# Pooled attention and a softplus feed-forward layer on one core: the scores of a chunk's two tiles in one interlude, the last keys transposed in one

## The chip, the cores and the metric

The kernel runs on one core of a Trainium2 chip. The metric is the device time of one execution in microseconds. The kernel before takes 896.08 us (median of 3 runs, 895.99 to 897.66). The core's engines are TensorE (PE; PEld is its weight load), VectorE (DVE), ScalarE (ACT), GpSimd (POOL) and SyncE (SP), which issues the DMAs.

## The reference

```python
# q, k, v: (8 batches, 8 heads, 576 tokens, 64), float32
k_p = k.reshape(B, H, Sp, pool, D).mean(axis=3)      # pool = 8, Sp = 72 pooled keys
v_p = v.reshape(B, H, Sp, pool, D).mean(axis=3)
scores = scale * np.matmul(q, k_p.transpose(0, 1, 3, 2))
scores = scores - np.max(scores, axis=-1, keepdims=True)
attn = np.exp(scores)
attn = attn / (np.sum(attn, axis=-1, keepdims=True) + 1e-09)
attn_out = np.matmul(attn, v_p)
x = attn_out.transpose(0, 2, 1, 3).reshape(4608, 512)
h = x @ w_in                                         # 512 x 2048
g = np.maximum(h, 0.0) + np.log1p(np.exp(-np.abs(h)))
out = g @ w_out                                      # 2048 x 512
```

## The kernel before

The 4608 tokens are worked through in 18 chunks (c = 0 to 17) of 256 tokens, each of two tiles of 128. A chunk first has its attention computed, which gives its rows of x, and then the feed-forward layer.

The feed-forward layer is most of the work. The 2048 hidden columns are taken in 8 pairs (u = 0 to 7) of two blocks of 128. To keep float32 accuracy, each operand is split in a high and a low part, and each product is three matmuls. For a pair, `pair1` (L582, tile h) makes the first products in 24 matmuls. ScalarE takes the softplus twice (L590, L604), VectorE forms low parts and sums of quarters (L611, L641 to L644, L660), and the second products follow. From chunk 4 (NF) on these are `pair2_fast` (L730, tile m): seven products of quarters instead of eight (a Strassen-like scheme), 21 matmuls, summed over the 8 pairs in four PSUM banks. They are made in the order 1, 2, 6, 7, 5, 3, 4. Product 4 is alone in its bank, so half of that bank is free. `finish` (L743, L751) puts a chunk's output together from the seven sums. Chunk 3 uses the plain `pair2` (L623).

The attention of a tile, in class `Tile`: `qT` transposes q in four transposes (L379), `qT_out` copies them out of PSUM; `scores` makes the scores of the eight heads (L399). A head has 64 dimensions and 64 rows of the tile are taken at a time, so four small matmuls share the array: two heads (j, the even and the odd half, each into its own bank) times two halves of the rows (i). In the profile each of them is two records, so a tile's scores are 32 records. `least` takes the row minimum (the scale is negative) of a bank's four heads (L406) and `less` subtracts it (L413), on VectorE. The exponential on ScalarE runs once for both tiles. Then come the row sums (L430), the reciprocal (L434, L435), `main` (L439) for the first 64 of the 72 keys and `ends` (L446) for the last 8. `ends` writes the products of the last 8 keys three times over, as 96 columns for each half of the heads, since they are used as high, low and high part: it is two VectorE instructions a tile. `PT` transposes the first 64 keys (L460, four transposes), `last` the last ones (L472, two transposes of 96 columns), `last_high` (L479) and `last_low` (L484) split them. `av_products` (L501, L508) multiplies with the values.

What sets the order. The whole order of work is made by a planner when the kernel is built, class `Order`. Every step is an `op` with an engine, a duration, steps that it waits for (`after`), and buffers (`Slot`s of a kind, as PSUM banks). It places steps one by one: it finds the engine whose next step could end first, and of that engine's steps that could start before this one's end and at most PAUSE (0.4 us) later than its first, it takes the one with the highest rank (longest path to the end, and a bonus `first`). `HOP` (0.15 us) is added for a step's result to reach another engine. The steps are then issued in order of planned start, and each engine works in that order; the framework sets the semaphores, and orders the accesses of different engines to a PSUM bank.

There are two lists: the first for the start of the kernel with chunks 0 to 2 and the attention of chunk 3, the second for the steady part (chunks 3 to 17). In the steady list, `steady_attention(c + 1)` is added while chunk c is in work, and products are planned at MM = 0.1195 us each. PSUM's eight banks are there two for h, four for sums (kind "acc") and two for all of the attention (kind "bank"). The scores of a tile take both of the latter.

Of the kernel before, what the change touches and what calls it, by code (L numbers as in the profile page):

```python
# [30 lines left out]
class Order:  # L31
# [5 lines left out]
    AWAY = 20  # L37

    def __init__(self, kinds):
        self.ops, self.kinds, self.first, self.last, self.begin, self.table = [], kinds, 0, None, {}, None  # L40

    def op(self, engine, cost, fn, after=(), slots=(), lag=None, rest=0, first=0, table=None):
# [9 lines left out]
    def run(self):  # L52
        for o in reversed(self.ops):
            o.rank = o.cost + max([x.rank + o.lag for x in o.followers] + [o.rest])
        now = dict(self.begin)
        table = self.table

        def cost(o):
            return o.cost + (self.TABLE if o.table not in (None, table) else 0)

        free = {k: [(0, n) for n in names] for k, names in self.kinds.items()}
        left = {o.i: len(o.after) for o in self.ops}
        ready = [o for o in self.ops if not o.after]
        order = []
        while ready:
            best, could = None, []
            for o in ready:
                new = [x.kind for x in o.slots if x.name is None]
                if any(len(free[k]) < new.count(k) for k in set(new)):
                    continue  # L70
                t = max([now.get(o.engine, 0)]
                        + [x.end + (x.lag if x.engine != o.engine or x.lag > 1 else 0)
                           for x in o.after]
                        + [sorted(free[k])[new.count(k) - 1][0] for k in set(new)])
                could.append((t, o))
                if best is None or t + cost(o) < best[0]:
                    best = t + cost(o), o.engine
            by = min(t for t, o in could if o.engine == best[1]) + self.PAUSE
# [25 lines left out]
def pooled_attention_softplus_ffn(  # L104
# [266 lines left out]
    class Tile:  # L371
# [110 lines left out]
        def last_low(self, ps):  # L482
# [2 lines left out]
                out=o, in0=ps[R:2 * R, 0:2 * P].rearrange("p (a i) -> p a i", a=2),  # L485
                in1=o.bitcast(F32), op=ALU.subtract)

    def av_products(c, pss):

        pt, lt = pt_[c], last_[c]
        sp = [(b % 2, slice(lo - c * CT, hi - c * CT)) for lo, hi, b in spans(c * CT, (c + 1) * CT)]
        for g in range(2):
            for i, t in sp:
                for e in range(2):
                    for r, ps in enumerate(pss):
                        rows, n = slice(r * KM, (r + 1) * KM), 2 * g + e

                        nc.tensor.matmul(  # L501
                            out=ps[e * D:(e + 1) * D, g * CT + t.start:g * CT + t.stop],
                            lhsT=vs[i][rows, n], rhs=pt[rows, n, t],
                            start=g == 0 and t.start == 0, stop=False)
# [208 lines left out]
    def pair2_fast(c, u, which=(1, 2, 6, 7, 5, 3, 4)):  # L713
        if u == 0:
            for i in range(0, len(which), 2):
                b = psum.tile([P, DM], F32, tag=m_banks.pop(0), name="m")
                ms.setdefault(c, {}).update({n: b[:, j * O2:(j + 1) * O2]
                                             for j, n in enumerate(which[i:i + 2])})
        g, gh, gl = gs[c, u]
        so = ss[c, u][1]  # L720
        a = {n: (gh[:, i], gl[:, i]) for n, i in ((1, 0), (2, 2), (4, 1))}
# [504 lines left out]
    def steady_attention(c):  # L1226
        s_q, s_E, s_lt = Slot("q"), Slot("E"), Slot("lt_")
        tiles = [Tile(c, t) for t in range(T)]

        def load():  # L1230
            load_q(c)
        o_q = op(SYNC, 3.0, load, qT_done.get(c - 1, ()), [s_q], lag=2.4)
        subs = []
        qT_done[c], score_done[c], av_done[c], x_done[c] = [], [], [], []
        for x in tiles:
            sp = spans(x.first, x.first + P)
            s, s_qT, s_mn = Slot("bank"), Slot("qT"), Slot("mn")
# [3 lines left out]
            o = op(ACT, act(512), lambda x=x, s=s, n=s_qT: x.qT_out(s.tile, n.name),  # L1241
                   [o], [s, s_qT])
            last, ss = [], [Slot("bank"), Slot("bank")]
            p = op(PE, 0.7, lambda x=x, ss=ss: x.scores([bank(s, "sc") for s in ss]),
                   [o, *parts_of(sp, k_ready)], [s_qT, *ss], first=EARLY)
            score_done[c].append(p)
            for i, s in enumerate(ss):
                last = [op(DVE, 0.46, lambda x=x, i=i, s=s, n=s_mn: x.least(i, s.tile, n.name), [p, *last],
                           [s, s_mn])]

                def less(x=x, i=i, s=s):
                    if c not in e_:
                        new_E(c)
                    x.less(i, s.tile)
                subs.append(op(DVE, 0.46, less, last, [s, s_mn, s_E]))
        return lambda where: probabilities(c, tiles, s_E, s_lt, subs, where)

    def probabilities(c, tiles, s_E, s_lt, subs, where):

        s_pT, lows = Slot("pT"), []  # L1260
        ex = op(ACT, 1.2 + TABLE, lambda: exponential(e_[c]), [*subs, where], [s_E])
        op(ACT, TABLE, lambda: None, [ex], first=5000)
        for x in tiles:
            s_sm, s_pm, s_pe = Slot("sm"), Slot("G"), Slot("pe")
# [3 lines left out]
            e = op(DVE, 0.52, x.ends, [o], [s_E, s_sm, s_pe])  # L1268
            s, r = Slot("bank"), Slot("bank")
            o = op(PE, 0.45, lambda x=x, s=s: x.PT(bank(s, "ptp")), [m], [s, s_pm], first=EARLY)  # L1270
            lows.append(op(ACT, act(512), lambda x=x, s=s: x.PT_out(s.tile), [o], [s, s_pT]))
            o = op(PE, 0.15, lambda x=x, r=r: x.last(bank(r, "ltp")), [e], [r, s_pe], first=EARLY)
            h = op(ACT, act(256), lambda x=x, r=r: x.last_high(r.tile), [o], [r, s_lt])
            lows.append(op(DVE, dve2(256), lambda x=x, r=r: x.last_low(r.tile), [h], [r, s_lt]))

        def values(after=()):
            sp = spans(c * CT, (c + 1) * CT)
            ss = [Slot("bank"), Slot("bank")]
            o = op(PE, 1.55 if len(sp) == 1 else 2.1,
                   lambda: av_products(c, [bank(s, "avp") for s in ss]),  # L1280
                   [*lows, *parts_of(sp, v_ready), *after], [*ss, s_lt, s_pT], first=EARLY)
            av_done[c].append(o)
# [50 lines left out]
    banks_of, drained = {}, {}  # L1333

    def second_products(c, u, before):
        fast = c >= NF
# [19 lines left out]
        elif u in (0, FP - 1):  # L1356
# [2 lines left out]
            o = p2[c, u] = op(PE, 9 * MM, lambda: fn((5, 3, 4)), [i, o], [*slots, *banks[2:]])  # L1359
            if u == FP - 1:  # L1360
                output(c, [i, o], banks)
        else:
            o = p2[c, u] = op(PE, 21 * MM, fn, wait, [*slots, *banks])
        return o
# [91 lines left out]
```

## Time and profile before

| what | value |
|---|---|
| median of 3 runs | 896.08 us |
| profiled execution, its own time | 899.16 us |
| its span, first to last instruction | 897.4 us |
| mean granted TensorE clock | 0.996 |
| TensorE busy | 884.9 us (99%) |
| first products L582, matmuls and busy time | 2880, 354.2 us |
| second products L730, matmuls | 2352 |
| scores L399, records and busy time | 1152, 27.2 us |
| transposes of the last keys L472 | 72, 14.0 us |

The span is the time between the first and the last instruction of one profiled execution; what the execution takes beyond it lies before and after. Busy time of TensorE counts each matmul from start to end, and matmuls overlap, so the sum over rows is more than the time that they hold the path. The chain of work that ended last gives each piece's share of the path, and is the better view here: its rows add up.

### The profile page before, as it was taken

What the parts mean: (1) busy time and instruction counts of PE and PEld (TensorE: products, weight loads), DVE (VectorE), ACT (ScalarE), POOL (GpSimd) and SP (SyncE); (2) the same over time, 40 slices, a digit from 0 to 9 for tenths busy, and PEclk for the clock granted to TensorE, in tenths of its full rate; (3) what the DMA queues carried; (4) which work ended last, traced back from release to release, by engine and by line L of the source; (5) the groups of instructions that cost most, each with busy time, mean ns of one, the idle gap of its engine ahead of it and who ended that gap; (6) DMA issues with size and microseconds to landing.
All of it is one profiled execution on the core that took longest, in us unless ns stands there. A gap on an engine that the chain in (4) does not pass through costs nothing.

```text
span 897.4 us, 20505 instructions
## 1 busy us (share of the span) xinstructions
PE 884.9 (99%) x8308; PEld 836.9 (93%) x8308; DVE 649.4 (72%) x1601; ACT 408.0 (45%) x824; POOL 2.4 (0%) x19
## 2 busy tenths in 40 slices
PE   7999999999999999999999999999999999999997
PEld 4789989888999999999999999999999999999997
DVE  5899999888867678787677666777566565747454
ACT  4964333445353544454444444353545354434332
POOL 1000000000000000000000000000000000000000
PEclk8999999999999999999999999999999999999999
DMA  8975545545897678687668775776656565747472
GB/s 247 283 245 179 198 144 166 171 156 180 283 291 232 225 244 263 201 267 235 211 199 256 230 221 190 221 245 219 221 171 229 188 212 190 234 142 228 173 241 88
DMA packets 107085, 191.12 MB, mean 213 GB/s; under 512 B 46064, under 2 KB 60400, under 8 KB 106992
## 3 DMA queue, kind: packets, MB, share of 16 engines
q1 hardware_dynamic: 106992, 189.82, 65.3%
q8 instruction: 65, 1.06, 0.5%
q14 instruction: 28, 0.23, 0.1%
HBM read 167.25 MB, written 22.54 MB: 211 GB/s over the span
## 4 chain that ended last, share of the span: by engine, by line
PE 95%; DMA 2%; DVE 1%; ACT 1%; SPq 0%; issue 0%; DVEq 0%; ACTq 0%
PE h L582 36%; PE m L730 30%; PE acc L556 7%; PE h L534 7%; PE acc L623 3%; PE sc L399 2%; PE avp L501 2%; PE qTp L379 2%; PE ptp L460 2%; PE avp L508 2%; DMA l<-wi 1%; PE ltp L472 1%; PE kps L965 1%; DMA kvl<-in_v_dram 1%; DMA kvst<-in_k_dram 0%; ACT E L424 0%
## 5 line engine op out<-in xcount | busy, mean ns | idle before, releaser
L582 PE MATMUL h<-x,l 128*128 128x256 f32 x2748 | 337.6, 279 | 0.5 <-DMA l<-wi 0.5
L582 PEld LDWEIGHTS h<-x,l 128*128 128x128 f32 x2748 | 323.8, 188 | 1.2 <-DMA l<-wi 0.7
L590 ACT ACTIVATE g<-h 128x512 f32<-128x512 f32 x120 | 71.9, 599 | 281.4 <-PE h L582 281.3
L730 PE MATMUL m<-w,so 128*128 128x256 f32 x1134 | 147.8, 277 | 0.0
L730 PEld LDWEIGHTS m<-w,so 128*128 128x128 f32 x1134 | 137.8, 188 | 0.1
L641 DVE TENSOR_TENSOR sf<-g 128x128 f32<-128x128 f32 x112 | 32.7, 292 | 127.4 <-ACT g L590 126.8
L655 ACT CAST so<-sf 128x512 fp32r<-128x512 f32 x112 | 69.7, 623 | 58.0 <-DVE sf L644 56.8
L660 DVE TENSOR_TENSOR so<-sf,so 128x512 fp32r<-128x512 f32 x112 | 77.4, 691 | 23.0 <-ACT so L655 22.9
L730 PE MATMUL m<-w,gh 128*128 128x256 f32 x476 | 91.5, 281 | 0.0
L730 PEld LDWEIGHTS m<-w,gh 128*128 128x128 f32 x476 | 71.9, 188 | 0.0
L611 DVE TENSOR_TENSOR gl<-g,gh 128x384 fp32r<-128x384 f32 (+1 forms) x120 | 67.3, 561 | 0.4 <-ACT gh L604 0.4
L730 PE MATMUL m<-w,gl 128*128 128x256 f32 x238 | 66.0, 277 | 0.0
L604 ACT ACTIVATE gh<-h 128x384 fp32r<-128x384 f32 (+1 forms) x120 | 59.1, 492 | 0.0
L539 ACT ACTIVATE g<-h 128x256 fp32r<-128x256 f32 x96 | 32.0, 382 | 55.4 <-PE h L534 33.5
L534 PEld LDWEIGHTS h<-x,w 128*128 128x128 f32 x396 | 48.6, 188 | 2.7 <-ACT g L539 0.6
L534 PE MATMUL h<-x,w 128*128 128x256 f32 x396 | 49.8, 278 | 0.2 <-ACT g L539 0.2
L730 PEld LDWEIGHTS m<-w,gl 128*128 128x128 f32 x238 | 44.7, 188 | 0.0
L751 DVE TENSOR_TENSOR o<-o,m 128x256 f32<-128x256 f32 x98 | 39.8, 418 | 3.3 <-ACT o L743 0.4
L556 PE MATMUL acc<-w,g 128*128 128x512 f32 x132 | 41.9, 399 | 0.0
L730 PE MATMUL m<-l,gh 128*128 128x256 f32 x196 | 39.9, 292 | 0.0
L406 DVE TENSOR_REDUCE mn<-sc 128x4 f32<-128x288 f32 x72 | 31.4, 451 | 7.9 <-PE sc L399 7.6
L644 DVE TENSOR_TENSOR sf<-g,sf 128x128 f32<-128x128 f32 x112 | 32.7, 292 | 3.9
(198 smaller groups left out, 1252.8 us busy)
## 6 DMA issues: line engine op xcount, KB each, us to landing
l<-wi SPq DMA_DIRECT2D x224, 512.0 KB
out_dram<-o SPq DMA_DIRECT2D x36, 256.0 KB
q<-in_q_dram SPq DMA_DIRECT2D x32, 256.0 KB
kst<-in_k_dram SPq DMA_DIRECT2D x24, 288.0 KB
vst<-in_v_dram SPq DMA_DIRECT2D x24, 256.0 KB
stage<-in_moe_w_in_dram SPq DMA_DIRECT2D x22, 256.0 KB
stage<-in_moe_w_out_dram SPq DMA_DIRECT2D x11, 512.0 KB
wi<-w SPq DMA_DIRECT2D x11, 512.0 KB
```

The lines of the kernel that those rows point to most:

```text
L534: nc.tensor.matmul(out=ps[:, 0:CT], lhsT=row(w, kc), rhs=x[:, kc], start=first and kc == j == 0, stop=last and kc == KC - 1 and j == 2)
L556: nc.tensor.matmul(out=accs[c][t], lhsT=a[:, ts], rhs=w, start=f == 0 and j == 0, stop=f == FC - 1 and j == 2)
L582: nc.tensor.matmul(out=ps[:, k * CT:(k + 1) * CT], lhsT=row(w, kc), rhs=x_[c][i][:, kc], start=first and n == 0, stop=last and n == len(or ...
L590: nc.scalar.activation(out=g, in_=x.rearrange("p (b i) -> p b i", i=P), func=AF.Softplus)
L604: nc.scalar.activation(out=gh, in_=quarters(c, x.rearrange("p (b i) -> p b i", i=P)), func=AF.Softplus)
L611: nc.vector.tensor_tensor(out=gl, in0=quarters(c, g), in1=gh.bitcast(F32), op=ALU.subtract)
L641: tt(out=sf[:, 2], in0=g[:, 0], in1=g[:, 2], op=ALU.add)
L644: tt(out=sf[:, 3], in0=g[:, 3], in1=sf[:, 1], op=ALU.subtract)
L655: nc.scalar.copy(out=so[:, 0], in_=ss[c, u])
L660: nc.vector.tensor_tensor(out=so[:, 1], in0=sf, in1=so[:, 0].bitcast(F32), op=ALU.subtract)
L730: nc.tensor.matmul(out=ms[c][n], lhsT=x, rhs=y, start=u == 0 and j == 0 and n in (1, 6, 5, 4), stop=u == FP - 1 and j == 2 and n in (2, 7, ...
L751: nc.vector.tensor_tensor(out=o, in0=in0, in1=m[n], op=how)
```

## The change

It touches the second (steady) list.

- The scores of both tiles of a chunk are one step, `pair_scores`, and take three banks instead of two at a time for each tile. The bank of half j takes seven heads (tile 0's four and tile 1's first three); the two heads left, tile 1's last pair, go in the first 144 columns of a third bank. For chunks 4 and 5 the third is a bank of kind "acc"; from chunk 6 on it is the free half of the bank of product 4 of chunk c - 2 (`ms[...]["rest"]`), written without the flag that starts a sum.
- The order of the scores' matmuls is: tile 1's last even head, all of tile 0, the rest of tile 1, tile 1's last odd head. A GpSimd memset of a small tile waits for the first of these, and the last of these waits for the memset.
- Minima and subtractions follow the banks: `pair_least` three times (two over 504 elements, one over 144), `pair_less` seven times, in place of four and four. The third bank's come first, with the bonus HURRY.
- The last keys: `pair_ends` writes each tile's products once (128x64, one VectorE instruction a tile), `pair_last` transposes both tiles' in one step of two transposes, `pair_high` makes the copies of the high part in four ScalarE copies (two of a tile's `last_high` before), `pair_low_ends` the low part in two.
- Durations in the list: MM is 0.1142 us instead of 0.1195, PAUSE for TensorE is 0.1 us instead of 0.4, av_products 1.7 and 2.15 instead of 1.55 and 2.1.

```diff
+    def pair_scores(c, tiles, pss):
+        rest, own = pss[2]
+        last = HP - 1
+        order = [(tiles[1], last, 0), *((tiles[0], m, j) for m in range(HP) for j in range(2)),
+                 *((tiles[1], m, j) for m in range(last) for j in range(2)), (tiles[1], last, 1)]
+        for x, m, j in order:
+            js, n, ps = slice(j * D, (j + 1) * D), HP * x.t + m, pss[j]
+            third = n == 2 * HP - 1
+            if third:
+                n, ps = j, rest
+            for i in range(2):
...
+                o = nc.tensor.matmul(out=ps[r, n * SP:(n + 1) * SP], lhsT=x.q[js, m, r],
+                                     rhs=kT[b % 2][js, m], start=own or not third, stop=True,
+                                     skip_group_check=third)
+                if third and not j:
+                    wrote = o
+                elif third:
+                    tc.add_manual_dep(o.ins, between.ins.name, order_dep, reason="bank")
+            if third and not j:
+                between = nc.gpsimd.memset(between_out, 0.0)
+                tc.add_manual_dep(between.ins, wrote.ins.name, order_dep, reason="bank")
...
+    def pair_ends(c, x, tag):
+        if c not in pe_:
+            pe_[c] = one.tile([P, T, H, KL], F32, tag="pe", name="pe")
+        nc.vector.tensor_tensor(out=pe_[c][:, x.t], in0=e_[c][:, x.t, :, KM:SP],
+                                in1=x.sm.unsqueeze(2).to_broadcast([P, H, KL]), op=ALU.mult)
+    def pair_last(c, ps):
+        for t in range(T):
+            nc.tensor.transpose(out=ps[0:2 * R, t * P:(t + 1) * P],
+                                in_=pe_[c][:, t].rearrange("p h k -> p (h k)"), identity=ident)
...
+    todo.pause = {PE: 0.1}
-    MM = 0.1195
+    MM = 0.1142
...
-            p = op(PE, 0.7, lambda x=x, ss=ss: x.scores([bank(s, "sc") for s in ss]),
-                   [o, *parts_of(sp, k_ready)], [s_qT, *ss], first=EARLY)
...
+        old = c - 2 if c - 2 >= NF else None
+        ss = [Slot("bank"), Slot("bank"), Slot("acc") if old is None else banks_of[old][3]]
+        p = op(PE, 1.4, lambda: pair_scores(
+            c, tiles, [*(bank(s, "sc") for s in ss[:2]), (third_bank(), old is None)]),
+               [*x_q, *parts_of(sp, k_ready), m_begun.get(old)], [*s_qT, *ss], first=EARLY)
+        for j in (2, 0, 1):
+            o = op(DVE, 0.3 if j == 2 else 0.68,
+                   lambda j=j, ps=ps: pair_least(c, j, ps(), s_mn.name), [p], [ss[j], s_mn],
+                   first=HURRY if j == 2 else 0)
+            for part in range(1 if j == 2 else 3):
+                subs.append(op(DVE, 0.3 if j == 2 else (0.46, 0.3, 0.22)[part],
+                               lambda j=j, ps=ps, part=part: pair_less(c, j, part, ps()), [o],
+                               [ss[j], s_mn, s_E], first=HURRY if j == 2 else 0))
...
-            o = op(PE, 0.15, lambda x=x, r=r: x.last(bank(r, "ltp")), [e], [r, s_pe], first=EARLY)
-            h = op(ACT, act(256), lambda x=x, r=r: x.last_high(r.tile), [o], [r, s_lt])
-            lows.append(op(DVE, dve2(256), lambda x=x, r=r: x.last_low(r.tile), [h], [r, s_lt]))
+        s_l = Slot("bank")
+        p = op(PE, 0.23, lambda: pair_last(c, bank(s_l, "ltp")), es, [s_l, s_pe], first=EARLY)
+        for a in range(2):
+            h = op(ACT, act(256), lambda a=a: pair_high(c, a, s_l.tile, a), [p], [s_l, s_lt])
+            lows.append(op(DVE, dve2(256), lambda a=a: pair_low_ends(c, a, s_l.tile), [h], [s_l, s_lt]))
+        for a in range(2):
+            lows.append(op(ACT, act(256), lambda a=a: pair_high(c, a, s_l.tile, 2), [p], [s_l, s_lt]))
```

More of the change, by code (lines that the diff above doesn't have):

```diff
@@ L77, in run @@
                     best = t + cost(o), o.engine
-            by = min(t for t, o in could if o.engine == best[1]) + self.PAUSE
+            by = min(t for t, o in could if o.engine == best[1]) + self.pause.get(best[1], self.PAUSE)
             t, o = max(((t, o) for t, o in could if o.engine == best[1] and t < min(best[0], by)),
@@ L486, in last_low @@
                 in1=o.bitcast(F32), op=ALU.subtract)
+    order_dep = mybir.DependencyInfo(mybir.DependencyClass.Sync, mybir.DependencyReason.DATA)
+    between_out = small.tile([P, 8], F32, tag="between", name="between")
+    def pair_scores(c, tiles, pss):
[9 more added lines that the diff above has]
+            for i in range(2):
+                r = slice(i * P // 2, (i + 1) * P // 2)
+                b = (x.first + i * P // 2) // S
+                o = nc.tensor.matmul(out=ps[r, n * SP:(n + 1) * SP], lhsT=x.q[js, m, r],
[8 more added lines that the diff above has]
+                tc.add_manual_dep(between.ins, wrote.ins.name, order_dep, reason="bank")
@@ L488, in av_products, with pair_high, pair_low_ends @@
+    def pair_high(c, a, ps, row):
+        if c not in last_:
+            last_[c] = one.tile([3 * R, 2, CT], F32R, tag="Y", name="lt_")
+        nc.scalar.copy(out=last_[c][row * R:(row + 1) * R, a], in_=ps[a * R:(a + 1) * R, 0:CT])
+    def pair_low_ends(c, a, ps):
+        rows, to = (slice(i * R, (i + 1) * R) for i in (a, 1 - a))
+        nc.vector.tensor_tensor(out=last_[c][to, a], in0=ps[rows, 0:CT],
+                                in1=last_[c][rows, a].bitcast(F32), op=ALU.subtract)
     def av_products(c, pss):
@@ L1234, in steady_attention @@
         qT_done[c], score_done[c], av_done[c], x_done[c] = [], [], [], []
-        for x in tiles:
-            sp = spans(x.first, x.first + P)
-            s, s_qT, s_mn = Slot("bank"), Slot("qT"), Slot("mn")
+        sp, s_mn, x_q = spans(c * CT, (c + 1) * CT), Slot("mn"), []
+        s_qT = [Slot("qT") for _ in tiles]
+        for x, n in zip(tiles, s_qT):
+            s = Slot("bank")
             o = op(PE, 0.45, lambda x=x, s=s: x.qT(bank(s, "qTp")), [o_q, *av_done.get(c - 1, ())],
```

59 lines of the change are left out of this document (41 added, 18 removed).

## The prediction

> **What bounds the kernel now.** I read the head of the page first, then the waits of TensorE, then the chain of work that ended last through one chunk of the steady part, then the other engines in the same stretch.
>
> ```profile
> span 897.4 us, 20505 instructions
> ...
> PE 884.9 (99%) x8308; PEld 836.9 (93%) x8308; DVE 649.4 (72%) x1601; ACT 408.0 (45%) x824; POOL 2.4 (0%) x19
> ...
> PE 95%; DMA 2%; DVE 1%; ACT 1%; SPq 0%; issue 0%; DVEq 0%; ACTq 0%
> ```
>
> TensorE is busy 99% of the span and is 95% of the chain. A busy TensorE could still hide waits, so the next view lists who kept it idle between 240 and 890 us, which is nearly the whole steady part (first line below), and how busy the others were in one chunk's time (second line: PE, PEld, DVE, ACT, POOL, clock, DMA share, GB/s).
>
> ```profile
> PE h L582 <- DMA l<-wi: 0.5, 1, 0.5
> 641.00:688.00 47.00, 47.00 (x482) 46.28 (x482) 30.49 (x84) 21.56 (x39) 0.00 (x0) 1.00 0.60 196
> ```
>
> One wait of 0.5 us in 650 us: there is no stall left to remove. VectorE has 16.5 us of 47 free, ScalarE 25.4, and the granted clock is full. Time can only go if TensorE gets less to do, and anything that makes it wait shows in full. What its work is, the chain shows (start, us on the path, what), here for one chunk:
>
> ```profile
> 689.66 0.87 PE ptp L460 x8
> 690.53 2.74 PE h L582 x24
> 693.27 0.22 PE ltp L472 x2
> 693.49 2.48 PE m L730 x21
> 695.97 0.22 PE ltp L472 x2
> 696.19 2.83 PE h L582 x24
> 699.02 1.02 PE avp L501 x16
> ...
> 703.12 0.87 PE qTp L379 x8
> 703.99 2.73 PE h L582 x24
> 706.72 0.66 PE sc L399 x32
> 707.38 2.67 PE m L730 x21
> 710.05 2.83 PE h L582 x24
> 712.88 0.66 PE sc L399 x32
> 713.54 2.60 PE m L730 x21
> 716.14 2.72 PE h L582 x24
> 718.86 2.38 PE m L730 x21
> ```
>
> The last two rows are undisturbed blocks: 24 first products in 2.72 us and 21 second products in 2.38. Between other blocks stands an interlude of attention work. It costs twice: its own row, and the surplus of the blocks behind it. After the first scores the m block takes 2.67 instead of 2.38 (+0.29) and the h block 2.83 instead of 2.72 (+0.11); after the second scores m takes 2.60 (+0.22). So the number of interludes counts, not only what stands in them.
>
> **The change part by part.** It is made in the steady list alone. The rows that count its instructions (form, count, busy us, mean ns), and the scores' own rows (first: shortest, median and longest matmul in ns; second: the group of 32 in the timeline):
>
> ```profile
> L413 DVE TENSOR_TENSOR E<-sc,mn 128x288 f32<-128x288 f32 x60 | 24.6, 449 | 0.1
> L406 DVE TENSOR_REDUCE mn<-sc 128x4 f32<-128x288 f32 x72 | 31.4, 451 | 7.9 <-PE sc L399 7.6
> L446 DVE TENSOR_TENSOR pe<-E,sm 128x96 f32<-128x96 f32 x72 | 15.3, 254 | 26.8 <-PE ltp L472 26.8
> L430 DVE TENSOR_REDUCE sm<-E 128x8 f32<-128x576 f32 x30 | 21.2, 748 | 17.8 <-ACT E L342 17.8
> L399 PE MATMUL sc<-kT,qT x1152: 222/223/379, 12.7 to 807.6; 64*64 64x72 f32 x192
> 706.65 0.73 PE L399 MATMUL sc<-kT,qT 64*64 64x72 f32 x32
> ```
>
> L413 runs 4 times a chunk, so x60 is 15 chunks; one of them (chunk 3) belongs to the first list, and 14 are in reach of the change.
>
> *Scores, two interludes into one.* Now: 0.66 + 0.29 + 0.11 + 0.66 + 0.22 = 1.94 us a chunk. After: one interlude of 64 records. The first 32 cost the 0.66 of the row; a further 32 cost what lies between the first and the last start, 0.73 - 0.22 = 0.51, and one pitch more, 0.53. The surplus behind it is paid once: 0.22 at least (as behind the second scores), 0.40 at most (as behind the first), 0.31 taken. The new order begins and ends with half a group (tile 1's last head pair, its even half first, its odd half last, so that the third bank is written by the two halves far apart in time), and the last half waits for a GpSimd memset. The trace has no half group: below, 0 (records alone count); above, 0.22, the row of the shortest interlude, two transposes; taken 0.12, about midway, since the half groups lie inside an interlude already begun. Sum 0.66 + 0.53 + 0.31 + 0.12 = 1.62, between 1.39 and 1.81. **Saved 0.32 us a chunk (0.13 to 0.55).** The Trainium skill (TensorE: Matmul & The Clock Gate, section Packing small matmuls — row/col tiling) says that small matmuls run at once only on different tiles of the array, and speaks against half groups. By it two more slots of four records would be paid, an estimate from the 0.51 us for eight pairs of such slots of about 0.13 us, so the gain by this rule would be 8.3 us in all, by the records alone 10.1.
>
> *Last keys, two interludes into one.* Now 0.22 + (2.48 - 2.38) + 0.22 + (2.83 - 2.72) = 0.65. After: two transposes in all, with 64 instead of 96 columns, 0.22 + 0.10 = 0.32; saved 0.33. In other chunks the transposes already stand together with the ptp ones, and then less can be saved:
>
> ```profile
> 502.46 0.22 PE ltp L472 x2
> 502.68 0.44 PE ptp L460 x4
> 503.11 2.40 PE m L730 x21
> 505.51 0.22 PE ltp L472 x2
> 505.73 2.75 PE h L582 x24
> ```
>
> Here the second costs 0.22 + 0.03 and the first no more than its 0.22: saved 0.22 to 0.25. **Taken 0.28 a chunk (0.22 to 0.33).**
>
> *VectorE and ScalarE.* Minima: four of 0.45 become two over 504 elements (below the 0.75 of the 576-element reduction; the list says 0.68) and a small one; subtractions: four of 0.45 become seven, two of the same size and five smaller, so between 0.9 and 3.1 us (the list plans 2.3); the padded products of 128x96, four of 0.25, become two of 128x64. All in all VectorE gets some 0.5 us more by the list's figures, ScalarE two more copies; both are hidden by the free 16.5 and 25.4 us, unless they come late. The places where late counts, with the rows of this chunk:
>
> ```profile
> 696.23 0.37 ACT L479 CAST lt__9477<-ltp 96x256 fp32r<-96x256 f32 x1 [0.49 <-PE ltp L472]
> 703.59 1.08 ACT L386 COPY qT<-qTp 128x512 f32<-128x512 f32 x2 [1.48 <-PE qTp L379]
> 714.96 1.39 DVE L751 TENSOR_TENSOR o<-o,m 128x256 f32<-128x256 f32 x3
> 716.87 1.66 DVE L751 TENSOR_TENSOR o<-o,m 128x256 f32<-128x256 f32 x4
> 718.44 0.45 DVE L406 TENSOR_REDUCE mn<-sc 128x4 f32<-128x288 f32 x1
> 1.64 0.10 POOL L165 MEMSET zl<- 128x8 f32 x1
> ```
>
> The merged scores wait for both qT copies; these end at 704.67, the scores start at 706.72, so 2.05 us cover them. The four ScalarE copies of the last keys (at most 4 x 0.37 = 1.48) from 696.23 on would end at 697.7; the av products come at 699.02, and 1.3 us are left. If that cover went, the av products could still move back a block, since h of the next chunk starts only at 710.05. The GpSimd memset took 0.10 us, and 0.26 us passed from the start of two transposes (695.97) to the copy that waited for them (696.23). Twice that and the memset make 0.62; the last half group comes 56 records, some 0.9 us, after the first. So the fence is hidden by the other scores; behind the waiting half group only the next block of products is queued. GpSimd's queue is otherwise empty, and no DMA is added or moved past.
>
> *The list.* A product is now planned at 0.1142 us instead of 0.1195: 24 make 2.74 instead of 2.87, against 2.72 on the chain. As TensorE does not wait now, a truer plan has nothing to gain on the chip, but it places the interludes anew. Split or joined transposes are worth 0.11 each time (an h block behind a lone half: 2.83). Taken at 0, bounds 1.5 us either way over 14 chunks.
>
> *Sum.* 14 x (0.32 + 0.28) = **8.4 us**; ends 14 x (0.13 + 0.22) = 4.9 and 14 x (0.55 + 0.33) = 12.3. The profiled execution took 899.16 us (span 897.4, 1.8 around it), so its like would take 890.8. The median of the runs shown is 3.1 us lower, 896.08: **887.7 us**, 883.8 to 891.2 by the bounds.
>
> **The rivals.**
>
> *Slower: the third bank holds up VectorE and so the next chunk's products.* The third bank is the free half of the bank in which product 4 of the chunk before the current one is summed. The drain on VectorE of these scores stands in the list with the same haste as the steps that drain that chunk's sums (L751). Now these end at 718.53; the first products into the freed banks are the 13th of the block at 718.86, at 718.86 + 12 x 0.113 = 720.22: 1.7 us to spare. If the merged scores fall in front of the old chunk's last block (where the second scores stand), up to 3.9 us of their VectorE work (the list's 0.3 + 0.3 + 2 x 1.66) competes with that drain. With all of it ahead TensorE waits 2.2 us a chunk; from 0.60 us on the gain is gone. With half of that, 1.1 us, the time is 896.08 - 8.4 + 15.4 = 903. For it: no other cover, and a wait is paid 14 times. Against it: the row at 718.44 shows the scores' minimum placed behind the drain, the two whole banks keep no haste, and the hasty part is only 0.6 us. The Trainium skill (PSUM — Partial Sum Buffer, section PSUM bank collisions raise a hardware error) forbids two engines in one bank and quadrant even at different columns. By that rule VectorE's reading must be kept apart from product 4's matmuls, so a minimum listed behind a block of the old chunk would wait for its end; no row of the trace shows it. Chance 0.10.
>
> *No change: the fence is late.* If GpSimd, idle since the start, answers not in 0.6 but in 1.5 us, TensorE waits 0.6 us in each merged interlude and all 8.4 us are lost: 896. For it: its only rows are from the start. Against: its queue is empty. Chance 0.06.
>
> *Faster, but by less: more cuts.* The new list sets the qT and ptp transposes apart in all chunks and leaves a short wait of 0.15 us each: 1.5 + 2.1 = 3.6 us less. From the middle, 887.7, that gives 891.3, from the low end, 891.2, 894.8; taken 893. Chance 0.08.
>
> **How the numbers follow.** The forecast has 0.76, the rivals 0.10, 0.06 and 0.08. Differences under 0.2% (1.8 us) can't be told from none. Faster by more: 0.76 + 0.08 = 0.84; within: 0.06; slower: 0.10. The range takes in the bounds of the forecast and reaches over the 893 of the smaller gain: 883.8 to 893.7.
>
> **What would show it.** Right: in the chain one sc row of 64 records a chunk of about 1.2 us, one ltp row of 0.22, the surplus once behind each; still no TensorE wait above 1 us in the steady part; a chunk some 0.6 us shorter. Wrong: TensorE waiting for VectorE at a second product's first block (the slower rival), an idle piece inside the sc row before its last records, released by GpSimd (the fence), or sc as long as 1.8 us.

## The result, and the profile after

The changed kernel takes 889.1 us (median of 4 runs, 887.0 to 891.26), the kernel before 896.81 us (4 runs): 7.7 us less by the medians. The ratio of the runs is 0.9909 (95% interval 0.9891 to 0.9926), which would be 8.2 us. Forecast were 8.4 us less and 887.7 us. The profiled execution of the changed kernel took 888.88 us, against 899.16 for that of before. The head of its page, and the share of the chain by engine:

```profile
span 887.2 us, 20509 instructions
...
PE 873.3 (98%) x8280; PEld 830.8 (94%) x8280; DVE 646.4 (73%) x1601; ACT 416.6 (47%) x852; POOL 3.8 (0%) x33
...
PE 95%; DMA 2%; DVE 1%; ACT 1%; issue 0%; SPq 0%; DVEq 0%; ACTq 0%
```

TensorE still bounds the kernel. The waits of TensorE between 240 and 890 us are again a single one, on a weight transfer:

```profile
PE h L668 <- DMA l<-wi: 1.0, 1, 1.0
```

The two spans differ by 10.2 us, more than the medians. The rows of the first products say why. First the kernel before (the second row of each is most of chunk 3, with which the steady part begins; the numbers behind the durations are the first and the last start), then the kernel after:

```profile
L582 PE MATMUL h<-x,l x2748: 276/276/387, 216.6 to 887.5; 128*128 128x256 f32 x197
...
L582 PE MATMUL h<-x,w x132: 276/276/386, 184.5 to 217.9; 128*128 128x256 f32 x132
```

```profile
L668 PE MATMUL h<-x,l x2748: 275/276/389, 212.8 to 877.3; 128*128 128x256 f32 x197
...
L668 PE MATMUL h<-x,w x132: 275/276/384, 181.4 to 214.1; 128*128 128x256 f32 x132
```

From the first to the last of these products, 887.5 - 184.5 = 703.0 us became 877.3 - 181.4 = 695.9: 7.1 us less, and that is the change. The other 3.1 us lie ahead of 184.5 us, in the first list, which the change doesn't touch; they belong to these two executions.

The chain through the chunk with the scores at 607 us (start, us on the path, what; m L508 are the third bank's records, m L817 the second products):

```profile
607.23 0.21 PE m L508 x2
...
607.50 0.87 PE sc L508 x42
...
608.38 0.06 PE m L508 x3
608.44 2.94 PE h L668 x24
611.38 2.38 PE m L817 x21
613.76 2.72 PE h L668 x24
...
635.63 2.74 PE h L668 x24
638.38 0.22 PE ltp L561 x2
638.60 2.41 PE m L817 x21
641.00 2.72 PE h L668 x24
```

One interlude of scores lasts from 607.23 to 608.44, 1.21 us, and costs 2.94 - 2.72 = 0.22 behind it; the next block is undisturbed. One ltp row of 0.22 stands where there were two, with 2.41 - 2.38 = 0.03 behind it.

The same scores in the timeline, with GpSimd and VectorE:

```profile
607.16 0.28 PE L508 MATMUL m<-kT,qT 64*64 64x72 f32 x2
...
607.63 0.10 POOL L516 MEMSET between<- 128x8 f32 x1 [45.83 <-PE m L508]
...
608.15 0.22 PE L508 MATMUL m<-kT,qT 64*64 64x72 f32 x1
...
609.01 0.30 DVE L530 TENSOR_REDUCE mn<-m 128x2 f32<-128x144 f32 x1
609.34 0.31 DVE L546 TENSOR_TENSOR E<-m,mn 128x144 f32<-128x144 f32 x1
```

From the start of the first half group to the end of the memset 607.73 - 607.16 = 0.57 us pass (0.62 was estimated), and the last half group starts 0.42 us after that. The fence is hidden. VectorE reads the third bank first.

But four of the fourteen chunks look otherwise. Here is the chain behind the scores at 421 us, which stand in the middle of an h block:

```profile
422.92 1.61 PE h L668 x12
424.53 2.47 PE m L817 x21
427.00 2.83 PE h L668 x24
```

Nothing waits, and yet each m block takes 2.47 instead of 2.38 us and each h block 2.83 instead of 2.72: the products follow each other at 118 ns instead of 113. So it goes on for five m blocks and four h blocks, until the ptp transposes at 448.21. Against 1.36 for the 12 products, 2.38 and 2.72, these rows and those like them sum to 1.15 us of surplus, 0.93 more than the 0.22 above. The chunks whose scores begin at 280, 421, 468 and 701 us are the four.

For comparisons over the whole steady part I add up what the interludes cost in each profile: the time from the end of the last product's pitch ahead of an interlude to the first product behind it, and all that later product pitches have above 113.3 ns (233.4 for the 512-wide products of chunk 3). Two interludes at the start, which still hold products of the first list, are left out. Before that is 90.6 us in 102 interludes, after 83.4 in 79. By kind: scores 27.5 to 25.2, transposes (q, keys, probabilities and their last keys) 36.5 to 31.7, av products 26.5 to 26.5.

### The profile page after: what moved, and what is told of

It reads as the page before. It is cut to its first block, busy times and chain, and to the rows that moved or that the text cites. A ratio compares the mean times of both kernels' runs of the same rounds, so it can differ in the third digit from the quotient of the medians.

```text
span 887.2 us, 20509 instructions
## 1 busy us (share of the span) xinstructions
PE 873.3 (98%) x8280; PEld 830.8 (94%) x8280; DVE 646.4 (73%) x1601; ACT 416.6 (47%) x852; POOL 3.8 (0%) x33
## 4 chain that ended last, share of the span: by engine, by line
PE 95%; DMA 2%; DVE 1%; ACT 1%; issue 0%; SPq 0%; DVEq 0%; ACTq 0%
PE h L668 37%; PE m L817 30%; PE acc L642 8%; PE h L620 7%; PE acc L709 3%; PE avp L587 2%; PE qTp L380 2%; PE ptp L461 2%; PE sc L508 1%; PE avp L594 1%; DMA l<-wi 1%; ACT E L425 1%; DMA kvl<-in_v_dram 1%; PE m L508 0%; PE sc L400 0%; PE ltp L561 0%
## 5 line engine op out<-in xcount | busy, mean ns | idle before, releaser
L817 PE MATMUL m<-w,so 128*128 128x256 f32 x1134 | 148.4, 278 | 0.0
L817 PEld LDWEIGHTS m<-w,so 128*128 128x128 f32 x1134 | 138.3, 188 | 0.1
L817 PE MATMUL m<-w,gh 128*128 128x256 f32 x476 | 92.0, 282 | 0.0
L817 PEld LDWEIGHTS m<-w,gh 128*128 128x128 f32 x476 | 72.1, 188 | 0.0
L817 PE MATMUL m<-w,gl 128*128 128x256 f32 x238 | 66.2, 278 | 0.0
L817 PEld LDWEIGHTS m<-w,gl 128*128 128x128 f32 x238 | 44.9, 189 | 0.0
L817 PE MATMUL m<-l,gh 128*128 128x256 f32 x196 | 38.1, 283 | 0.0
L431 DVE TENSOR_REDUCE sm<-E 128x8 f32<-128x576 f32 x30 | 21.2, 748 | 18.3 <-ACT E L343 18.3
```

The lines of the kernel that those rows point to most:

```text
L817: nc.tensor.matmul(out=ms[c][n], lhsT=x, rhs=y, start=u == 0 and j == 0 and n in (1, 6, 5, 4), stop=u == FP - 1 and j == 2 and n in (2, 7, ...
```

## The experiments

My theory: the gain is that of fewer interludes, some 4 us each from scores and last keys; the fence and VectorE's work are hidden; the new durations in the list bring nothing. Rivals: the list alone makes the gain; the fence or the third bank costs something that hides in the rows; and, once the four slow chunks were seen, three reasons for them: where the scores stand, chance, or how the interlude ends.

**The parts alone.** Three kernels divide the change. The first is the kernel before with only the new durations (those of the av products too):

```diff
+    todo.pause = {PE: 0.1}
-    MM = 0.1195
+    MM = 0.1142
```

> The changed list durations alone (a product planned at 0.1142 us, TensorE's pause 0.1 us, the av products 1.7 and 2.15 us); scores and last keys as before. Theory (the time goes where interludes of TensorE go, and the list alone removes none): between 1.5 us faster and 1.5 us slower than before, no TensorE wait above 1 us in the steady part. Rival (the truer list carries part of the 8 us by placing interludes better): 2 to 4 us faster than before, with fewer interludes or a smaller surplus behind them.

It took 899.11 us against 898.48, ratio 1.0014 (1.0001 to 1.0027). The new list has 109 interludes instead of 102: it splits transposes that stood together. Alone it gains nothing and loses 0.0014 x 898 = 1.3 us, by the interval 0.1 to 2.4.

The second is the changed kernel with the old scores, one step for each tile; the third has the new scores and the old last keys:

```diff
-        p = op(PE, 1.4, lambda: pair_scores(
...
+            p = op(PE, 0.7, lambda x=x, ss=ss: x.scores([bank(s, "sc") for s in ss]),
```

> The new list durations and the last keys transposed in one step; the scores stay two interludes a chunk. Theory: the prediction's term of 0.28 us a chunk, 14 x 0.28 = 3.9 us faster than the list alone (3.1 to 4.6); by the changed kernel's chain, where the joined transposes cost 0.22 + 0.03 instead of 0.65, up to 14 x 0.40 = 5.6 us. Rival (the later ScalarE copies hold up the av products, so that TensorE waits): under 2 us faster than the list alone, with TensorE waiting for the copies.

```diff
-        p = op(PE, 0.23, lambda: pair_last(c, bank(s_l, "ltp")), es, [s_l, s_pe], first=EARLY)
...
+            o = op(PE, 0.15, lambda x=x, r=r: x.last(bank(r, "ltp")), [e], [r, s_pe], first=EARLY)
```

> The new list durations and the merged scores; the last keys stay two interludes a chunk with padded copies. Theory: by the changed kernel's chain a merged interlude costs 1.21 + 0.22 = 1.43 us instead of 1.94, so 14 x 0.51 = 7.1 us faster than the list alone, less 0.93 us for every chunk in which the products behind the scores keep a pitch of 118 ns instead of 113 over ten blocks (four chunks in the changed kernel: 3.4 us faster). Rival (the prediction's size, 0.32 us a chunk everywhere): 4.5 us faster with no such stretch.

With the last keys alone it took 894.65 us, ratio 0.9957 (0.9942 to 0.9972), with the scores alone 895.82 us, 0.9968 (0.9950 to 0.9986). Both have the new list, so they are set against the first kernel: 0.9957 / 1.0014 = 0.9943 makes 5.1 us for the last keys, 0.9968 / 1.0014 = 0.9954 makes 4.1 us for the scores. Forecast were 3.9 and 4.5. The intervals of two such ratios leave about 1.8 us of doubt in each, so the shares are shown, but not which is the larger. The list's 1.3 us off, the sum is 7.9 us, which is the whole change.

The slow pitch is in both. The kernel with the new scores has three long stretches, behind the scores at 471, 659 and 707 us, and so has the one that keeps the old scores: behind its second scores at 289, 570 and 665 us some 190 to 200 products follow each other at 118 ns. The last of them in its chain:

```profile
664.76 0.66 PE sc L400 x32
665.42 2.67 PE m L817 x21
668.09 2.83 PE h L668 x24
670.91 2.47 PE m L817 x21
```

So a long stretch doesn't need merged scores. With the new list alone there is one, behind the second scores at 569 us.

**The place of the scores.** In the slow chunks the scores stand between the two halves of the first h block. This kernel makes that block one step, so that no scores can stand in it:

```diff
+        if True:
-        if u == 0:
-            o = op(PE, 12 * MM, lambda: pair1(c, u, bank(s, "h"), range(0, KC, 2)), wait[:-1],
...
```

> The changed kernel, with a chunk's first block of first products planned as one step of 24 matmuls instead of two of 12, so that no interlude can stand inside it. In the changed kernel four of the six chunks whose scores stand inside that block keep the pitch of 118 ns for some 210 products behind them (0.93 us each), and none of the others. Theory (a place inside the block brings the slow pitch): no long slow stretch, 3 to 4 us faster than the changed kernel, 885 to 886. Rival (the pitch depends on something else, and the place is chance): slow stretches in other chunks, within 1.5 us of the changed kernel's 889.1.

It took 889.9 us, ratio 0.9913 (0.9891 to 0.9935), as the change itself. The scores now stand between whole blocks, and behind those at 423, 467 and 703 us the slow pitch is there all the same (behind those at 282 us too, up to the wait shown next, behind which the products run at 113 ns). That reason falls. Its only wait of TensorE in the steady part shows something else:

```profile
292.11 0.48 PE L817 MATMUL m<-w,gh 128*128 128x256 f32 x2 [1.37 <-DVE E L546]
```

Once in 14 chunks the old chunk's product 4 waited until VectorE had read the third bank, the free half of product 4's own bank.

**Chance.** The changed kernel itself, once more:

> The changed kernel once more, unchanged. It tells whether the stretches in slow pitch (118 ns a product over 210 products, behind the scores at 280, 421, 468 and 701 us of the first profile) belong to the program or to chance. Theory now (the pitch is set by how the first weight loads behind an interlude fall, which a few ns decide): stretches of this length again, some in other chunks than before. Rival (they belong to fixed chunks): the same four. Time: 7 to 9 us faster than before in both.

890.14 us, ratio 0.9916 (0.9899 to 0.9933). The slow chunks are those at 283, 423, 470 and 703 us, which are the same four. Chance falls: the slow pitch belongs to the program. There is no TensorE wait at all in the steady part of this profile.

**The fence laid open.** The scores in plain order, so that the two half groups stand next to each other with nothing between them to hide the memset:

```diff
+        order = [*((tiles[0], m, j) for m in range(HP) for j in range(2)),
+                 *((tiles[1], m, j) for m in range(HP) for j in range(2))]
-        order = [(tiles[1], last, 0), *((tiles[0], m, j) for m in range(HP) for j in range(2)),
-                 *((tiles[1], m, j) for m in range(last) for j in range(2)), (tiles[1], last, 1)]
```

> The changed kernel with the scores' matmuls in plain order, so that the two halves of the last head pair, with the GpSimd memset between them, stand next to each other. By the changed kernel's trace 0.58 us pass from the first record of the early half to the end of the memset. Theory (the fence is hidden only by the order): the last half starts some 0.5 us later behind all others, 14 x 0.5 = 7 us slower than the changed kernel, about 896. Rival (the fence costs what it costs wherever it stands): within 2 us of the changed kernel.

Its chain, and its waits:

```profile
610.92 1.04 PE sc L508 x56
611.96 0.14 PE m L508 x4
...
612.20 0.12 POOL between L516
...
612.36 0.34 PE m L508 x4
612.70 2.94 PE h L668 x24
```

```profile
PE m L508 <- POOL between L516: 3.5, 12, 0.3
```

The interlude takes 612.70 - 610.92 = 1.78 instead of 1.21 us, 0.57 more, and the chain runs through GpSimd. That is what the order of the changed kernel hides, and 14 x 0.57 = 8.0 us was to be expected. The time is 893.96 us, ratio 0.9962 (0.9945 to 0.9978): only 3.8 us more than the change in the same call, with about 2 us of doubt. By the sums over the steady part, against the second profile of the changed kernel, the interludes cost 7.9 us more and the pitches behind them 2.4 less: the four slow stretches are gone, and a new one stands behind the scores at 225 us, where the changed kernel has none. That leaves 5.5 us. So the way in which the interlude ends, or the wait in it, bears on the pitch behind it.

**The haste of the third bank.** VectorE reads the third bank last instead of first, and without the bonus:

```diff
-        for j in (2, 0, 1):
+        for j in (0, 1, 2):
...
-                   first=HURRY if j == 2 else 0)
```

> The changed kernel with the third bank's minimum and subtraction last and without their bonus, so that 3.3 us of VectorE work on the two whole banks may stand before them. This is the prediction's slower rival made stronger. Rival's mechanism: TensorE waits for VectorE at products into a bank of sums, 0.5 to 1.5 us in several chunks, 4 us or more slower than the changed kernel. Theory (there is cover left: in the changed kernel the third bank is read by 609.65, and the next matmul into that bank comes near 613.4): few such waits, under 3 us slower.

912.31 us, ratio 1.0165 (1.0145 to 1.0185): slower than the kernel before, and 22 us slower than the change. My theory of a few such waits falls, and the rival's mechanism is there. The waits (total, times, longest), and one of them in the timeline:

```profile
PE m L817 <- DVE E L546: 15.8, 9, 1.9
```

```profile
636.76 0.30 DVE L546 TENSOR_TENSOR E<-m,mn 128x144 f32<-128x144 f32 x1
637.21 0.47 PE L817 MATMUL m<-w,gh 128*128 128x256 f32 x2 [1.67 <-DVE E L546]
```

Nine times product 4 stands still for up to 1.9 us, since VectorE comes to the subtraction of the third bank only behind the softplus work and the other banks. The Trainium skill (PSUM — Partial Sum Buffer, section PSUM bank collisions raise a hardware error) asks that a PSUM bank be guarded as a whole in each group of 32 partitions, not by address. These waits are what such a guard costs here: the two use different columns of one bank, and one waits for the other. It is the framework that sets the waits; what the chip would do without them no run shows.

The waits are 15.8 of the 22 us. Most of the rest is the clock. Behind three of the nine waits, those of 1.86, 1.94 and 1.86 us that end at 295, 541 and 733 us, the granted clock falls to one half for 3.4 us, and the h block behind takes 4.15 to 4.36 us instead of 2.72. Two of them in the chain, and the clock behind the second, which is the 0.50 (the fields are length, PE, PEld, DVE, ACT, POOL busy, clock, DMA share, GB/s):

```profile
295.83 4.35 PE h L668 x24
...
541.39 4.36 PE h L668 x24
```

```profile
541.80:545.20 3.40, 3.40 (x18) 3.40 (x17) 0.00 (x0) 0.00 (x0) 0.00 (x0) 0.50 0.24 92
```

That is 1.6 us each time, 4.9 us in all. Behind the other six waits, two of them just as long (1.86 and 1.94 us), the clock stays at full speed. In this kernel a wait can cost almost twice its length.

**How the interlude ends.** First the last half group's two matmuls are issued twice, four records more; then only one of the two is:

```diff
-                 *((tiles[1], m, j) for m in range(last) for j in range(2)), (tiles[1], last, 1)]
+                 *((tiles[1], m, j) for m in range(last) for j in range(2)), (tiles[1], last, 1), (tiles[1], last, 1)]
```

```diff
-            for i in range(2):
+            for i in (0, 1, 1) if third and j else (0, 1):
```

> The changed kernel with the last half group of the scores made twice (the same values are written again), which adds four records of some 0.06 us to each interlude. Theory (phase behind an interlude decides the slow pitch): another set of chunks is slow; time 14 x 0.06 = 0.9 us slower, and then up to 3.7 us less or more as fewer or more chunks are slow. Rival (fixed chunks): the same four, 0.9 us slower.

> The changed kernel with the repeated half group, measured again in more rounds. By the chain the interlude is 0.12 us longer (14 x 0.12 = 1.7 us) and the surplus behind the interludes 3.9 us smaller: 2.2 us faster than the changed kernel, and no long slow stretch again in this execution. Rival (the one execution was lucky): slow stretches return, 1 to 2 us slower.

> The changed kernel with only one matmul of the last half group made twice (two records more, on one tile of the array). The repeated half group cost 0.12 us an interlude and took all long slow stretches away. Theory (a later end is enough): no long stretch, 0.06 to 0.12 us more an interlude, 2 to 3 us faster than the changed kernel. Rival (the second pass over both row halves is needed): stretches remain, 1 to 2 us slower than the changed kernel.

One thing in these expectations is wrong: the same values are not written again. From chunk 6 on the half group is written without the flag that starts a sum (`start=own or not third`), and a second matmul without it adds to the first, just as this kernel sums its second products. So the scores of that one head of tile 1 come out doubled (with the single matmul, for half of the tile's rows). Put into the reference, that moves its output by 0.9% of its norm (0.7%). These kernels show what another end does to the time; they don't compute what the change computes.

More work, less time: 887.96 us, ratio 0.9892 (0.9873 to 0.9910), for the half group twice, where the change in the same call had 0.9916. In a second call, where the change itself did not run, the same kernel gave 887.8 us, 0.9880 (0.9859 to 0.9900), and the single matmul more gave 887.25 us, 0.9886 (0.9866 to 0.9905). The chain of the latter, at the place shown above for the changed kernel:

```profile
421.61 1.57 PE h L668 x12
423.18 2.38 PE m L817 x21
425.56 2.72 PE h L668 x24
```

The slow pitch is gone, here and in the other three chunks, so one matmul more is enough. In the sums over the steady part, the half group twice costs 14 x 0.125 = 1.75 us more in the interludes and saves 3.9 in the pitches behind (13.0 to 9.05 us): 2.2 us less, and the medians differ by 890.14 - 887.96 = 2.2. The intervals of the two ratios still overlap; all three runs of this kind have a ratio below 0.99, and no other kernel here has. In the second profile of the half group twice the pitches behind cost 10.8 us and not 9.05: in one chunk TensorE waits 0.3 us for weights at 583 us, and the slow pitch starts behind that wait. The single matmul costs the same 0.125.

Then two kernels with other ends and no more work: the halves swapped (the odd head first, the even one last), and the two rows of 64 in turned order:

```diff
-        order = [(tiles[1], last, 0), *((tiles[0], m, j) for m in range(HP) for j in range(2)),
+        order = [(tiles[1], last, 1), *((tiles[0], m, j) for m in range(HP) for j in range(2)),
...
```

```diff
-            for i in range(2):
+            for i in (1, 0):
```

> The changed kernel with the two halves of the last head pair changing places in the order of the scores (odd half first, even half last). The same work in the same number of records and the same order on every other engine. Theory (the slow pitch hangs on how the end of the interlude falls against the first weight loads, whichever half ends): no saying which chunks; the stretches of 210 slow products may go, at best 3.7 us faster than the changed kernel. Rival (the stretch needs another length of interlude, as with the repeated half group): the same four chunks slow, time as the changed kernel's within 1 us.

> The changed kernel with the two halves of a tile's rows changing places in every pair of score matmuls. Same work, same order elsewhere. As for the swapped halves: theory, another set of slow chunks or none, up to 3.7 us faster; rival, the same four chunks slow and the same time within 1 us.

With the halves swapped the interlude gets 0.05 us shorter and the time longer: 893.33 us, ratio 0.9943 (0.9923 to 0.9963). Eight chunks are slow now: the rival's same four falls, and the gain that the theory held possible doesn't come. Behind the scores at 421 us:

```profile
423.89 2.47 PE m L817 x21
426.36 2.83 PE h L668 x24
```

With the rows turned it is 891.74 us, 0.9923 (0.9899 to 0.9947), and five slow chunks, the four and one at 657 us. So with all else as in the changed kernel, the last records of an interlude change how many chunks go slow: eight, five, four or none. They aren't the whole of it: with the same last records the kernel with the new scores and the old last keys has three, not all in the same chunks. Why the records matter, and why in some chunks and not in others, the runs don't show; it stays open.

## Why the prediction was right, point by point

*The bound.* Right: TensorE gets less to do, and the time falls by that. No new wait came. That the total is so near, 7.7 us where 8.4 were forecast, is in part luck: by the parts the last keys gave 1.2 us more than forecast, the scores 0.4 less and the list 1.3 less, and these cancel.

*Scores.* 0.32 us a chunk was forecast, from 1.94 to 1.62. The interlude was costed at 0.66 + 0.53 + 0.12 = 1.31 and takes 1.21: the half groups cost 1.21 - 0.66 - 0.53 = 0.02 us and not 0.12, next to the lower bound. By the rule of the Trainium skill (TensorE: Matmul & The Clock Gate, section Packing small matmuls — row/col tiling) that small matmuls run at once only on different tiles, I had estimated 0.13; the trace doesn't bear that estimate out. What falls is my reading that a half group leaves slots empty, not the rule itself, which no run here tests. The surplus was "paid once: 0.22 at least, 0.40 at most". It is 0.22 in the chunk shown and 0.22 + 0.93 in four others. That is the mis-sized term. I took the surplus for a price that one interlude pays once. The 2.83 of the row 710.05 quoted above was the slow pitch already: 24 products at 118 instead of 113 ns. In the kernel before, the second scores came one m and one h block later, and the slow pitch ended there; in these four chunks it goes on until the next interlude. That it goes on because an interlude was taken out is not shown, as the kernel with the old scores and the new last keys has such stretches too. With 1.43 in ten chunks and 2.36 in four the mean is 1.70, and the saving 0.24 instead of 0.32, or 3.4 us in all. The sums over the steady part give 2.3, or 2.8 without the waits on weights, and 3.3 with the second profile of the changed kernel, which has no such wait; the two kernels' times give 4.1 with the doubt named above. The prediction's lower sum was also added up wrong: 0.66 + 0.53 + 0.22 is 1.41 and not 1.39, which moves the low end of the forecast from 883.8 to 884.0 us.

*Last keys.* 0.28 a chunk forecast, 3.9 us; 5.1 by the kernels' times. The new interlude costs 0.22 + 0.03 = 0.25, where 0.22 + 0.10 was taken. The 1.2 us between lie within the doubt of 1.8. Part of them may be how the list places the transposes: the ptp transposes of both tiles stand joined in 10 chunks instead of 6. This I had left in the list's bounds.

*The list.* Forecast 0, within 1.5 us either way; alone it was 1.3 us slower.

*VectorE and ScalarE.* VectorE was to get 0.5 us more a chunk by the list's figures. They don't say so: minima 2 x 0.68 + 0.3, subtractions 2 x (0.46 + 0.3 + 0.22) + 0.3 and products 2 x 0.23 are 4.38 us, less than the 4.62 measured before. The groups of after (count, busy us, mean ns):

```profile
L530 DVE TENSOR_REDUCE mn<-sc 128x7 f32<-128x504 f32 x28 | 17.7, 672 | 0.0
L546 DVE TENSOR_TENSOR E<-sc,mn 128x288 f32<-128x288 f32 x28 | 12.1, 449 | 0.0
L546 DVE TENSOR_TENSOR E<-sc,mn 128x144 f32<-128x144 f32 x30 | 7.9, 297 | 0.1
L556 DVE TENSOR_TENSOR pe<-E,sm 128x64 f32<-128x64 f32 x28 | 5.8, 218 | 0.0
L546 DVE TENSOR_TENSOR E<-sc,mn 128x72 f32<-128x72 f32 x28 | 5.3, 222 | 0.0
L530 DVE TENSOR_REDUCE mn<-m 128x2 f32<-128x144 f32 x12 | 3.7, 308 | 16.6 <-PE m L508 16.6
L546 DVE TENSOR_TENSOR E<-m,mn 128x144 f32<-128x144 f32 x12 | 3.7, 308 | 0.4
```

Minima 2 x 0.672 + 0.308 = 1.65, subtractions 2 x (0.449 + 0.297 + 0.222) + 0.308 = 2.24, products 2 x 0.218 = 0.44: 4.33 us, against 4 x (0.449 + 0.451 + 0.254) = 4.62 before. It is 0.3 less, and hidden as said. ScalarE's four copies, in the chunk of the chain above:

```profile
639.34 0.73 ACT L567 CAST lt__8775<-ltp 32x256 fp32r<-32x256 f32 x2
640.86 0.75 ACT L567 CAST lt__8775<-ltp 32x256 fp32r<-32x256 f32 x2
```

They end at 641.61, and in the chain the next block of h runs until the av products at 643.72: no wait.

*The rivals.* Late fence: it is in time by 0.42 us, and 0.57 us an interlude is what it costs when open, so the rival named a real price and lacked its condition. More cuts: the ptp transposes stand joined more often, not less; the qT ones are split in four chunks. The slower rival: its mechanism is real. That the waits in the kernel without haste sum to 15.8 us, where 15.4 was worked out for half the full price, is chance: they are nine waits of 1.45 to 1.94 us and not fourteen of 1.1. And the place was wrong. It is not the drain of the sums that comes late for the next chunk's products; it is the old chunk's own product 4 that waits for VectorE's reading of the third bank, which I had put the other way round, as a minimum that waits for product 4. And what keeps it away is that the third bank is read first and with the bonus HURRY (the run took both away, so which of the two does it is not shown), not the free time of VectorE: VectorE is no busier than before (646.4 us against 649.4), and without the haste the kernel is slower than the one before.

## What to carry to other kernels

Where one engine is the bound and doesn't wait, count the interruptions of its main stream and not only their length, and take the price of one from the blocks behind it; but look how far it reaches: if the second block behind is longer too, the cost may last until something ends it. Where a new use shares a buffer with the main stream, the order in which the other engine frees it decides the sign: here it is 0.9% gained with the read put first and 1.6% lost with it last. After a merge, try a few ends of the merged step, as they moved the time by up to 6 us here; but see that the work stays the same. The ends that brought the gain from 0.9% to 1.1% also add to a sum, and an end of that kind that leaves the scores as they are was not run.

## What the runs showed of the hardware that was not expected

- The 128x256 products run at one of two pitches, 113 or 118 ns, with nothing waiting. The granted clock is the same in both stretches; below, the slow one at 422.9 us and the other at 608.4 us (length; then PE, PEld, DVE, ACT, POOL busy; clock; DMA share; GB/s). What the pitch is, is set at an interlude, can change at a wait (as at the two at 292 and 583 us above), and is kept to the next one. The Trainium skill (TensorE: Matmul & The Clock Gate, section Wait — 56ns, not 53.3ns?) gives the columns by 2.4 GHz and about 2.5 ns for a matmul at full clock, an estimate of 109 ns for 256 columns; the runs show more in both, and two values.

```profile
422.90:448.20 25.30, 25.30 (x217) 25.30 (x216) 21.23 (x60) 12.01 (x19) 0.00 (x0) 1.00 0.84 268
608.40:626.60 18.20, 18.20 (x163) 18.20 (x162) 12.79 (x38) 7.53 (x12) 0.00 (x0) 1.00 0.73 229
```

- In the slow stretch the DMA share is higher, 0.84 against 0.73. The kernel with one matmul more has 0.76 and 264 GB/s in the same place at the 113 ns pitch, so the transfers alone don't make it slow.
- Half groups of small matmuls cost 0.02 us for two, beside other such groups; four more records at the end of the interlude cost 0.125 us, and two more just as much.
- In the kernel without haste the granted clock fell to one half for 3.4 us behind three of nine waits of TensorE of at most 1.94 us, which cost 1.6 us each time beyond the wait.
- A round from TensorE over a GpSimd memset of 0.10 us and back adds 0.57 us to the interlude when nothing covers it.
